# One fused compare-and-multiply on VectorE in the last attention batch, products on GpSimd elsewhere, and flags by maxima

## The chip, the cores and the metric

The kernel runs on one core of one Trainium2 chip. The metric is the device time in microseconds, the median of several executions. Engines are named as the profile does: PE is TensorE, DVE is VectorE, ACT is ScalarE, POOL is GpSimd, SP is the queue from which most transfers are issued.

## The reference

Four batches of eight heads, 576 positions and head size 64 go through attention that keeps the 32 largest scores of each row; its output (2304 rows of 512) goes through a mixture of eight experts, two for each row.

```python
scores = scale * np.matmul(q, k.transpose(0, 1, 3, 2))
kth = np.partition(scores, -32, axis=-1)[..., -32:-31]
scores = np.where(scores >= kth, scores, -1000000000.0)
attn = np.exp(scores - np.max(scores, axis=-1, keepdims=True))
attn = attn / (np.sum(attn, axis=-1, keepdims=True) + 1e-09)
x = np.matmul(attn, v)                                # then (2304, 512)
noisy = x @ w_gate + np.log1p(np.exp(x @ w_noise)) * noise
...                                                   # the two largest, softmaxed
out[mask] += top2_w[mask, k, None] * (np.maximum(x[mask] @ w1[e], 0.0) @ w2[e])
```

## The kernel before

**Attention.** A batch is 36 tiles of 128 query rows, 144 tiles in all (`attend`, `finish`, `gather`). For a tile, PE computes 576 scores in two halves (L577 for the first batch, L581 for the others), and ACT copies them to SBUF as `s` (L589). DVE folds the two halves into maxima and minima (L612) and finds the 32 largest in four rounds of eight (MAX8 at L616, with the found ones struck out at L621 between rounds). In some tiles (24 of 144, `DROPS`) ACT and POOL strike out the third eight; these leave one value each in `left` and `apart`. ACT takes the exponential of all scores, `es` (L644), which needs only the maximum; `es` has four buffers. The 32nd value decides which are kept: either DVE writes a mask `mk` of ones and zeros (`mask`, L648), or a threshold `under` (L678, on DVE or POOL) and a sign pass on ACT (L682) write it. `SIGNS` says how many tenths of the tiles of each batch take the second way: 10, 10, 6 and 4. Then `weigh` multiplies `es` by the mask (L693): on POOL, or on DVE where the planner finds that this is earlier by a margin (`WEIGHS`). POOL notes in `over` how the 32nd value stands to the rounds before (`note`, L696). PE transposes the product (L708, L712) and multiplies it with the values (L768, L770); ACT and DVE or POOL scale the rows by their sums (L789, L795, L803).

**Routing.** After each batch, `gate` computes the logits (L865, last part added by DVE at L881), and `route` computes gates, ranks and slots with small instructions on ACT, DVE and POOL; then ten indirect DMAs on POOL's queue scatter the rows into lists of each expert (L1044).

**Experts.** They run in three groups of rows: the first after batch 0, the second (256 rows of each expert) after batch 2, the third after batch 3. Each block of weights is loaded from HBM, rounded by ACT (`wh`, L1112), and the rest is taken by a subtraction on POOL or DVE (`wl`, L1116, 128x1024, two for each half-block). PE multiplies in three passes (L1200 to L1202 up, L1282 to L1284 down). Between the two, ACT writes the relu `hh` (L1206) and DVE the rest `hl` (L1210, a scalar_tensor_tensor with one operand in PSUM); for the inputs the same are L1170 and `xl` (L1173). An indirect DMA on POOL adds the result into the output (L1302). The experts of the second group are interleaved with the attention of the last batch.

**Order.** Each piece of work is a node with an engine, a duration, dependencies and a priority (low numbers first). `Plan.order` simulates the engines and lists the pieces in order of their planned start; each engine executes its own in that order. A node with `alt` may move to a second engine. Nodes with `lock=True` on DVE and POOL do not start in the plan while one of the other engine runs. Buffers are rings (`take`, `give`) that add dependencies.

**Flags.** Four reasons could make the fast path wrong; `bad` counts them, and at the end `bad` decides whether a general path runs instead. `flags(b)` (L1006 to L1020) counts them for one batch: for each of the three columns of `over`, for `under`, and for `left` and `apart` where the batch has any, a comparison into `fl` (L1018), a sum (L1019) and an addition to `bad` (L1020). That is 20 such groups. The four calls have the lowest priority of all and depend on every tile's note, so they come after the last tile.

Of the kernel before, what the change touches and what calls it, by code (L numbers as in the profile page):

```python
# [8 lines left out]
F32 = mybir.dt.float32  # L9
# [5 lines left out]
OP = mybir.AluOpType  # L15
# [16 lines left out]

SIGNS = (10, 10, 6, 4)


WEIGHS = (1500, 1600, 2300, 1900)
BIAS = (400, 300, 800, -1100)
BELOW = (1300, -2500, 2200, 2600)  # L40
LOWK = (2300, 400, 500, 1300)
# [17 lines left out]

TAKE = ((0, 208), (48, HS), (0, HS))  # L60
GLAG = 1

WHEN = (16, 15, -13, 0)

# [363 lines left out]
def sparse_attention_moe(ctx: ExitStack, tc: tile.TileContext, qk, v, wg, aux, noise, w1, w2, out):  # L428
# [62 lines left out]
    def qkv(n):  # L491
        b, h = divmod(n, H)

        def whole():
            hi[n] = P["hi"].tile([128, QW + KW], F32, name="hi", bufs=4)
            nc.sync.dma_start(hi[n][0:64], qk[b, h])
            vt[n] = P["v"].tile([128, 6, 65], F32, name="vt", bufs=NV)
            nc.sync.dma_start(vt[n], v[b, h])

        if b < NATIVE:  # L500
            a = add("SP", 1000, whole, move=1330, lat=700)
            QN[n] = (a, a, a, pl.take("hi", 4, a), None, pl.take("v", NV, a))
            return

        def load():
            raw[n] = P["raw"].tile([128, QW + KW], F32, name="raw", bufs=2)
            nc.sync.dma_start(raw[n][0:64], qk[b, h])
            nc.sync.dma_start(raw[n][64:128], qk[b, h])
            vt[n] = P["v"].tile([128, 6, 65], F32, name="vt", bufs=NV)
            nc.sync.dma_start(vt[n], v[b, h])  # L510

        def high():
            t = P["hi"].tile([128, QW + KW], F32, name="hi", bufs=4)
            hi[n] = t.bitcast(F32R)
            nc.scalar.activation(hi[n], raw[n], AF.Copy)

        def low_k(eng):
            kl[n] = P["kl"].tile([128, KW], F32R, name="kl", bufs=4)
            ENG[eng].tensor_tensor(kl[n], raw[n][:, QW:], hi[n][:, QW:].bitcast(F32), op=OP.subtract)

        def low_q(eng):
            ENG[eng].tensor_tensor(hi[n][64:128, :QW], raw[n][64:128, :QW], hi[n][64:128, :QW].bitcast(F32), op=OP.subtract)

        a = add("SP", 1500, load, move=2200, lat=2500)
        r, vv = pl.take("raw", 2, a), pl.take("v", NV, a)
        x = add("ACT", 1165, high, [a])
        hh = pl.take("hi", 4, x)
        y = add("POOL", 1545, low_k, [x], alt=("DVE", 736, LOWK[b]), lock=True)
        kk = pl.take("kl", 4, y)
        z = add("POOL", 1625, low_q, [x], alt=("DVE", 850, LOWK[b]), lock=True)  # L530
        pl.give(r, y, z)
        QN[n] = (a, y, z, hh, kk, vv)
# [18 lines left out]
    def attend(j):  # L551
# [129 lines left out]
            t["mk"] = W.tile([128, S], BF, name="mk", bufs=NMK)  # L681
            nc.scalar.activation(t["mk"], t["s"], AF.Sign, bias=under[:, j:j + 1])  # L682

        if sgn:
            k = add("DVE", 71, below, [d], alt=("POOL", 179, BELOW[b]))
            mk = add("ACT", 667, sign, [k])
        else:
            mk = add("DVE", 430, mask, [d], lock=True)
        bk = pl.take("mk", NMK, mk)
        pl.give(t["sbuf"], mk, x2)  # L690

        def weigh(eng):
            ENG[eng].tensor_tensor(t["e"], t["e"], t["mk"], op=OP.mult)  # L693

        def note():
            nc.gpsimd.tensor_tensor(over[:, j], t["t8"][:, 3, 7:8].to_broadcast([128, 3]), t["t8"][:, 0:3, 7], op=OP.subtract)  # L696

        w = add("POOL", 1240, weigh, [mk, x2], alt=("DVE", 669, WEIGHS[b]), lock=True)
        pl.give(bk, w)
        nt_ = add("POOL", 150, note, [mk])  # L700
        pl.give(b8, nt_, x1, k if sgn else mk, n2 or nt_)
        t["note"] = nt_

        def turn():
# [205 lines left out]
    def route(b):  # L910
# [92 lines left out]
                V.tensor_reduce(new("c0", [1])[:n], st["tm"][:n, 0, a:z, 8], axis=AX.X, op=OP.add)  # L1003
                V.tensor_tensor(bad[:n, 0:1], bad[:n, 0:1], st["c0"][:n], op=OP.add)

        def flags(b):  # L1006
            fl = R.tile([128, 36], F32, name="flg")
            fr = R.tile([128, 1], F32, name="fr")
            q = slice(b * 36, (b + 1) * 36)
            p = [sides.index(j) for j in range(b * 36, (b + 1) * 36) if j in sides]  # L1010
            p = slice(p[0], p[-1] + 1) if p else None
            for x, c, op in ((over[:, q, 0], 0.0, OP.is_gt), (over[:, q, 1], 0.0, OP.is_gt), (over[:, q, 2], 0.0, OP.is_gt),
                             (under[:, q], -2.0 ** -100, OP.is_gt), (left[:, p], HS - 15.0, OP.not_equal) if p else (None,) * 3,
                             (apart[:, p], 0.0, OP.is_le) if p else (None,) * 3):
                if x is None:
                    continue
                n = x.shape[1]
                nc.vector.tensor_scalar(fl[:, :n], x, c, None, op0=op)  # L1018
                nc.vector.tensor_reduce(fr, fl[:, :n], axis=AX.X, op=OP.add)  # L1019
                nc.vector.tensor_tensor(bad[:, 0:1], bad[:, 0:1], fr, op=OP.add)  # L1020

        x0 = add("ACT", 130, ex, [AVN["lgn", b]])
        pr = pl.take("route", 1, x0)
# [28 lines left out]

        for t in range(NT):
            for k in range(2):
                scat.append(add("POOL", 1280, scatter(t, k), [x, g, AVN["tok", b]] + [(s, True) for s in scat[-1:]] + FILLS, move=750, lat=700))
        y = add("DVE", 75, cnt, [x])
        ck = add("DVE", 1000, check, [x, od], prio=pl.prio + 150)
        if b == B - 1:
            for i in range(B):
                add("DVE", 2590, lambda i=i: flags(i), [T[j]["note"] for j in range(36 * B)], prio=10 ** 9)  # L1060
        pl.give(pr, x, y, ck, g)
        pl.give(AVN["xrp", b], scat[-1])
        pl.give(AVN["axp", b], x2, AVN["tok", b])
# [403 lines left out]
```

## Time and profile before

| what | us |
|---|---|
| median of 3 executions | 998.77 |
| lowest, highest | 997.01, 1000.16 |
| profiled execution, its own time | 1007.95 |
| its span, first to last instruction | 1006.2 |
| mean granted PE clock | 0.973 of full speed |

The profile is that of one execution, and the hardware profiler's times are of single instructions. The tiles of the last batch run from about 457 to 731 us of the span, its flags and routing after them up to about 773 us, and the rest is the end of the second and the third group of experts. The granted clock is a share of 2.4 GHz; about 0.5 is the lower level, 1.2 GHz.

### The profile page before, as it was taken

The numbers are of one execution on the slowest core, as the hardware profiler recorded it, in microseconds if no ns is written. First come the engines' busy times: TensorE is split into PE (matmuls) and PEld (weight loads), VectorE is DVE, ScalarE is ACT, GpSimd is POOL, SyncE is SP. The second block draws the span as 40 slices with busy tenths as digits, with TensorE's granted clock in tenths as the row PEclk, the third lists the DMA queues.
The fourth block names the chain that finished last, engine by engine and source line by source line (L and its number), as shares of the span: only waits on it lengthen the run. The fifth ranks groups of instructions, "written<-read, shape, count | busy, mean of one in ns | idle before, by whom it ended". The sixth has DMA issues, their size and how long they took to land.

```text
span 1006.2 us, 18439 instructions
## 1 busy us (share of the span) xinstructions
PE 940.1 (93%) x6160; PEld 788.6 (78%) x6176; DVE 695.3 (69%) x2190; ACT 680.0 (68%) x1533; POOL 742.4 (74%) x926
## 2 busy tenths in 40 slices
PE   9999998899999899999699999899978999999993
PEld 4777776787887677888489988799867888999892
DVE  6999998799999799999783578877784222222220
ACT  5888885688987478887476668577635555555550
POOL 4676677355657666677689889687858899999991
PEclk9999999799998999999999999999979999999997
DMA  9477222157366664566667677354556877776741
GB/s 281 162 259 258 49 70 93 28 155 214 125 175 175 234 172 113 154 188 149 217 231 220 168 199 191 96 159 137 137 158 206 245 215 232 233 226 211 230 126 25
DMA packets 109385, 173.92 MB, mean 173 GB/s; under 512 B 7648, under 2 KB 60896, under 8 KB 109280
## 3 DMA queue, kind: packets, MB, share of 16 engines
q1 hardware_dynamic: 100576, 152.42, 48.8%
q0 software_dynamic: 8704, 20.22, 9.7%
q8 instruction: 51, 0.84, 0.3%
q14 instruction: 54, 0.44, 0.1%
HBM read 136.34 MB, written 36.27 MB: 172 GB/s over the span
## 4 chain that ended last, share of the span: by engine, by line
PE 61%; DVE 11%; POOL 10%; ACT 7%; issue 5%; DMA 2%; another core or an unknown queue 1%; SPq 0%; POOLq 0%; DVEq 0%; ACTq 0%
PE bank L768 7%; PE hps L1200 4%; POOL wl L1116 4%; PE hps L1202 4%; PE hps L1201 4%; PE pp L708 4%; PE bk L577 4%; PE bk L581 4%; PE bk L1274 3%; PE bk L1284 3%; PE bk L1282 3%; DVE t L616 3%; PE bk L1283 3%; PE hps L1229 3%; PE hps L542 3%
## 5 line engine op out<-in xcount | busy, mean ns | idle before, releaser
L1116 POOL TENSOR_TENSOR wl<-wr,wh 128x1024 fp32r<-128x1024 f32 x118 | 292.6, 2717 | 26.6 <-ACT wh L1112 14.0
L616 DVE MAX8 t<-cat 128x8 f32<-128x288 f32 (+3 forms) x576 | 268.1, 490 | 9.4 <-POOL cat L630 6.7
L693 POOL TENSOR_TENSOR es<-es,mk 128x576 f32<-128x576 f32 x140 | 187.2, 1341 | 94.2 <-ACT mk L682 74.9
L1112 ACT ACTIVATE wh<-wr 128x1024 fp32r<-128x1024 f32 x128 | 133.7, 1056 | 51.1 <-PE bk L1284 25.4
L1210 DVE SCALAR_TENSOR_TENSOR hl<-hps,hh 128x256 fp32r<-128x256 f32 x128 | 53.8, 421 | 155.6 <-ACT hh L1206 152.8
L621 DVE MATCH_REPLACE8 cat<-t,cat 128x208 f32<-128x208 f32 (+2 forms) x408 | 159.9, 394 | 0.0
L1200 PE MATMUL hps<-xh,wh 128*128 128x256 f32 x512 | 149.9, 293 | 2.2 <-DVE hl L1210 2.2
L612 DVE TENSOR_TENSOR cat<-bk,s 128x288 f32<-128x288 f32 x288 | 125.5, 444 | 33.7 <-ACT s L589 33.5
L1202 PE MATMUL hps<-xh,wl 128*128 128x256 f32 x512 | 145.9, 285 | 0.5 <-POOL wl L1116 0.5
L1201 PE MATMUL hps<-xl,wh 128*128 128x256 f32 x512 | 145.8, 285 | 0.0
L768 PEld LDWEIGHTS bank<-vt,pt 128*128 128x128 f32 x1024 | 124.1, 196 | 15.1 <-ACT p L720 10.4
L768 PE MATMUL bank<-vt,pt 128*128 128x65 f32 x1024 | 126.3, 278 | 7.1 <-ACT p L720 7.0
L589 ACT ACTIVATE s<-bk 128x288 f32<-128x288 f32 x288 | 111.5, 416 | 31.8 <-PE bk L581 19.4
L644 ACT ACTIVATE es<-s,nb 128x576 f32<-128x576 f32 x144 | 111.7, 777 | 4.6 <-POOL nb L638 2.6
L716 ACT ACTIVATE pt<-pp 128x512 f32<-128x512 f32 x144 | 86.3, 599 | 33.8 <-PE pp L708 27.2
L1200 PEld LDWEIGHTS hps<-xh,wh 128*128 128x128 f32 x512 | 98.5, 192 | 4.6 <-DVE hl L1210 2.5
L1201 PEld LDWEIGHTS hps<-xl,wh 128*128 128x128 f32 x512 | 98.5, 192 | 2.0
L1202 PEld LDWEIGHTS hps<-xh,wl 128*128 128x128 f32 x512 | 98.3, 192 | 0.7 <-POOL wl L1116 0.7
L1206 ACT ACTIVATE hh<-hps 128x256 fp32r<-128x256 f32 x128 | 48.8, 381 | 70.6 <-PE hps L1202 66.2
L708 PE MATMUL pp<-ident,es 128*128 128x128 f32 x576 | 89.5, 278 | 7.1 <-POOL es L693 4.0
L682 ACT ACTIVATE mk<-s,under 128x576 bf16<-128x576 f32 x107 | 83.0, 780 | 16.4 <-POOL under L678 11.8
L581 PE MATMUL bk<-hi 128*128 128x288 f32 x240 | 90.0, 384 | 3.0 <-DVE cat L612 1.6
(155 smaller groups left out, 2048.0 us busy)
## 6 DMA issues: line engine op xcount, KB each, us to landing
wr<-in_w_dram SPq DMA_DIRECT2D x192, 512.0 KB, 4.7
raw<-in_qk_dram SPq DMA_DIRECT2D x48, 320.0 KB, 8.7
xg<-xs SPq DMA_DIRECT2D x16, 528.0 KB, 8.6
xs<-xg SPq DMA_DIRECT2D x16, 528.0 KB
vt<-in_v_dram SPq DMA_DIRECT2D x32, 195.0 KB, 6.3
out_dram<-xs SPq DMA_DIRECT2D x1, 5120.0 KB
hi<-in_qk_dram SPq DMA_DIRECT2D x8, 320.0 KB, 4.7
xg<-xs SPq DMA_DIRECT2D x8, 264.0 KB
```

The costliest lines, as they stand in the source:

```text
L581: nc.tensor.matmul(sp, lhs(n), rhs, start=(k == 0), stop=(k == 2 * len(heads) - 1))
L612: nc.vector.tensor_tensor(o, t["sp", 1], t["s"][:, :HS], op=op)
L616: return lambda: nc.vector.max(t["t8"][:, r], t["cat"] if r == 3 else t["cat"][:, slice(*TAKE[r])])
L621: nc.vector.match_replace(g, t["t8"][:, r], g, NEG)
L693: ENG[eng].tensor_tensor(t["e"], t["e"], t["mk"], op=OP.mult)
L708: nc.tensor.transpose(pp[:, c], t["e"][:, k0 + c * 128:k0 + (c + 1) * 128], ident)
L768: nc.tensor.matmul(accs[:, i + k], x["pt"][:, c], vt[n][:, c], start=(k + c == 0), stop=False, skip_group_check=True)
L1112: nc.scalar.activation(WS[n][0][:, i], W[n][:, i], AF.Copy)
L1116: return lambda eng: ENG[eng].tensor_tensor(WS[n][1][:, i], W[n][:, i], WS[n][0][:, i].bitcast(F32), op=OP.subtract)
L1200: nc.tensor.matmul(ps[:, :NN], ah, xh, start=(c == 0), stop=False)
L1201: nc.tensor.matmul(ps[:, :NN], ah, xl, start=False, stop=False)
L1202: nc.tensor.matmul(ps[:, :NN], al, xh, start=False, stop=(c == 3))
```

## The change

In batch 3 (`FUSED` has 10 tenths there and none elsewhere) one DVE instruction compares `s` with the 32nd value and multiplies by `es`, in place; no mask, no sign pass and no threshold are made there. In the other batches the product has POOL as its only engine. `flags` is called once: five reductions over all 144 tiles (the maximum of `over`, of `under` and of `left`, the minimum of `left` and of `apart`), then five one-element instructions that compare and add to `bad`. `SENDS` (all zeros) is added to the priority of the scatters.

```diff
+FUSED = (0, 0, 0, 10)
...
-WEIGHS = (1500, 1600, 2300, 1900)
...
+SENDS = (0, 0, 0, 0)
...
-        def low_k(eng):
+        def low_k(eng="POOL"):
...
-        if sgn:
-            k = add("DVE", 71, below, [d], alt=("POOL", 179, BELOW[b]))
-            mk = add("ACT", 667, sign, [k])
-        else:
-            mk = add("DVE", 430, mask, [d], lock=True)
-        bk = pl.take("mk", NMK, mk)
-        pl.give(t["sbuf"], mk, x2)
-
-        def weigh(eng):
-            ENG[eng].tensor_tensor(t["e"], t["e"], t["mk"], op=OP.mult)
+        def weigh():
+            nc.gpsimd.tensor_tensor(t["e"], t["e"], t["mk"], op=OP.mult)
+
+        def both():
+            nc.vector.scalar_tensor_tensor(t["e"], t["s"], t["t8"][:, 3, 7:8], t["e"], op0=OP.is_ge, op1=OP.mult)
+
+        if spread(j % 36, FUSED[b]):
+            k = w = mk = add("DVE", 690, both, [d, x2], lock=True)
+            pl.give(t["sbuf"], mk)
+        else:
+            if sgn:
+                k = add("DVE", 71, below, [d], alt=("POOL", 179, BELOW[b]))
+                mk = add("ACT", 667, sign, [k])
+            else:
+                k = mk = add("DVE", 430, mask, [d], lock=True)
+            bk = pl.take("mk", NMK, mk)
+            pl.give(t["sbuf"], mk, x2)
+            w = add("POOL", 1240, weigh, [mk, x2], lock=True)
+            pl.give(bk, w)
...
-        w = add("POOL", 1240, weigh, [mk, x2], alt=("DVE", 669, WEIGHS[b]), lock=True)
-        pl.give(bk, w)
         nt_ = add("POOL", 150, note, [mk])
-        pl.give(b8, nt_, x1, k if sgn else mk, n2 or nt_)
+        pl.give(b8, nt_, x1, k, n2 or nt_)
...
-        def flags(b):
...
+        def flags():
+
+            fr = R.tile([128, 5], F32, name="fr")
+            red = lambda k, x, op: lambda: V.tensor_reduce(fr[:, k:k + 1], x, axis=AX.XYZW if len(x.shape) > 2 else AX.X, op=op)
+
+            def sums():
+                for k, c, op in ((0, 0.0, OP.is_gt), (1, -2.0 ** -100, OP.is_gt), (2, HS - 15.0, OP.not_equal),
+                                 (3, HS - 15.0, OP.not_equal), (4, 0.0, OP.is_le)):
+                    V.scalar_tensor_tensor(bad[:, 0:1], fr[:, k:k + 1], c, bad[:, 0:1], op0=op, op1=OP.add)
+            notes = [T[j]["note"] for j in range(36 * B)]
+            fs = [add("DVE", 60 + n / .96, red(k, x, op), notes, prio=10 ** 9) for k, n, x, op in (
+                (0, 432, over.rearrange("p j k -> p (j k)"), OP.max), (1, 144, under, OP.max), (2, 40, left, OP.max),
+                (3, 40, left, OP.min), (4, 40, apart, OP.min))]
+            add("DVE", 600, sums, fs, prio=10 ** 9)
...
-                scat.append(add("POOL", 1280, scatter(t, k), [x, g, AVN["tok", b]] + [(s, True) for s in scat[-1:]] + FILLS, move=750, lat=700))
+                scat.append(add("POOL", 1280, scatter(t, k), [x, g, AVN["tok", b]] + [(s, True) for s in scat[-1:]] + FILLS,
+                                prio=pl.prio + SENDS[b], move=750, lat=700))
...
-            for i in range(B):
-                add("DVE", 2590, lambda i=i: flags(i), [T[j]["note"] for j in range(36 * B)], prio=10 ** 9)
+            flags()
```

## Rows read from the trace of the kernel before

**Rows 1.** The page, busy time of each engine

```profile
PE 940.1 (93%) x6160; PEld 788.6 (78%) x6176; DVE 695.3 (69%) x2190; ACT 680.0 (68%) x1533; POOL 742.4 (74%) x926
```

**Rows 2.** Windows: us, then busy PE, PEld, DVE, ACT, POOL; clock, DMA, GB/s

```profile
457.00:525.00 68.00, 59.22 (x373) 47.39 (x373) 55.78 (x184) 43.02 (x111) 48.93 (x74) 0.97 0.72 203
525.00:625.00 100.00, 98.00 (x705) 89.75 (x705) 61.19 (x176) 69.85 (x145) 89.62 (x75) 1.00 0.71 201
625.00:731.00 106.00, 100.46 (x719) 91.90 (x718) 85.81 (x219) 71.98 (x155) 85.87 (x81) 0.98 0.47 138
731.00:748.00 17.00, 11.26 (x71) 9.98 (x70) 15.56 (x58) 6.05 (x15) 9.58 (x8) 0.87 0.52 136
760.00:812.00 52.00, 47.84 (x305) 42.15 (x305) 14.05 (x28) 28.23 (x46) 46.74 (x42) 1.00 0.80 244
812.00:991.00 179.00, 177.11 (x1142) 159.44 (x1142) 37.55 (x89) 95.56 (x160) 164.98 (x102) 1.00 0.68 200
```

**Rows 3.** Chain of waits from 727 to 748 us, shares by line

```profile
by line: DVE bad L1020 49.0%; DVE fr L1019 18.7%; DVE flg L1018 15.2%; issue 6.6%; DVE hl L1210 5.2%; DVE xl L1173 3.1%; ACT hh L1206 1.9%; DVE lgs L881 1.1%; DVE rs L795 0.4%
```

**Rows 4.** Timeline of DVE and POOL during the flags: start, duration in us

```profile
727.74 0.75 DVE L1018 TENSOR_SCALAR flg<-over 128x36 f32<-128x36 f32 x1
...
729.78 2.18 DVE L1020 TENSOR_TENSOR bad<-bad,fr 128x1 f32<-128x1 f32 x1
...
732.31 1.96 DVE L1020 TENSOR_TENSOR bad<-bad,fr 128x1 f32<-128x1 f32 x1
...
741.31 3.56 DVE L1020 TENSOR_TENSOR bad<-bad,fr 128x1 f32<-128x1 f32 x1
...
747.22 0.16 DVE L1020 TENSOR_TENSOR bad<-bad,fr 128x1 f32<-128x1 f32 x1
...
729.55 4.71 POOL L1116 TENSOR_TENSOR wl<-wr,wh 128x1024 fp32r<-128x1024 f32 x2 [0.94 <-POOL over L696]
...
741.89 2.95 POOL L1116 TENSOR_TENSOR wl<-wr,wh 128x1024 fp32r<-128x1024 f32 x1
```

**Rows 5.** Timeline of PE during the flags: idle before, released by

```profile
735.65 0.44 PE L1166 MATMUL hps<-ident,xs 128*128 128x128 f32 x2 [1.73 <-DVE xl L1173]
...
748.28 0.80 PE L1284 MATMUL bk<-wh,hl 128*128 128x512 f32 x1 [4.29 <-DVE hl L1210]
```

**Rows 6.** Windows in which PE ran at the lower clock

```profile
736.50:740.20 3.70, 3.70 (x17) 3.37 (x16) 3.32 (x19) 2.33 (x4) 1.94 (x4) 0.54 0.80 264
748.30:754.00 5.70, 5.70 (x20) 5.08 (x21) 3.11 (x13) 0.70 (x3) 3.63 (x11) 0.52 0.44 157
```

**Rows 7.** Single lines: ns min/median/max, first and last start, forms

```profile
L1019 DVE TENSOR_REDUCE fr<-flg x20: 156/191/192, 728.5 to 747.0; 128x1 f32<-128x36 f32 x16, 128x1 f32<-128x21 f32 x2, 128x1 f32<-128x3 f32 x2
...
L693 DVE TENSOR_TENSOR es<-es,mk x4: 741/752/759, 164.2 to 338.4; 128x576 f32<-128x576 f32 x4
...
L1210 DVE SCALAR_TENSOR_TENSOR hl<-hps,hh x128: 400/425/427, 526.1 to 986.7; 128x256 fp32r<-128x256 f32 x128
...
L648 DVE TENSOR_SCALAR mk<-s,t x37: 490/510/2590, 302.3 to 724.0; 128x576 bf16<-128x576 f32 x37
```

**Rows 8.** Groups by line, 457 to 731 us: busy us, mean ns, idle before

```profile
L1116 POOL TENSOR_TENSOR wl<-wr,wh 128x1024 fp32r<-128x1024 f32 x44 | 110.3, 2573 | 20.9 <-ACT wh L1112 8.3 <-issue 8.1 <-POOL over L696 2.6
L693 POOL TENSOR_TENSOR es<-es,mk 128x576 f32<-128x576 f32 x38 | 53.4, 1407 | 14.8 <-DVE mk L648 7.3 <-ACT mk L682 6.3 <-PE bank L712 0.9
...
L648 DVE TENSOR_SCALAR mk<-s,t 128x576 bf16<-128x576 f32 x23 | 15.7, 686 | 0.2
```

**Rows 9.** Waits, 500 to 731 us: us in total, times, longest

```profile
PE pp L708 <- POOL es L693: 3.5, 4, 1.7
```

**Rows 10.** Timeline of POOL at the first scatter; window of L693 alone (DVE, POOL)

```profile
163.41 1.22 POOL L1044 DMA_INDIRECT xg<-xr,si  x1 [0.73 <-POOL spacer L1043]
...
175.17 0.91 POOL L1044 DMA_INDIRECT xg<-xr,si  x1 [0.25 <-issue]
...
160.00:200.00 40.00, 2.25 (x3) 3.85 (x3) 0.83 0.23 75
```

More of the change, by code (lines that the diff above doesn't have):

```diff
@@ L515, in high, with low_q @@
             nc.scalar.activation(hi[n], raw[n], AF.Copy)
-        def low_k(eng):
+        def low_k(eng="POOL"):
             kl[n] = P["kl"].tile([128, KW], F32R, name="kl", bufs=4)
             ENG[eng].tensor_tensor(kl[n], raw[n][:, QW:], hi[n][:, QW:].bitcast(F32), op=OP.subtract)
-        def low_q(eng):
+        def low_q(eng="POOL"):
             ENG[eng].tensor_tensor(hi[n][64:128, :QW], raw[n][64:128, :QW], hi[n][64:128, :QW].bitcast(F32), op=OP.subtract)
@@ L1004, in check @@
                 V.tensor_tensor(bad[:n, 0:1], bad[:n, 0:1], st["c0"][:n], op=OP.add)
-        def flags(b):
[L1007 to L1020, printed above, removed]
+        def flags():
[10 more added lines that the diff above has]
+            add("DVE", 600, sums, fs, prio=10 ** 9)
         x0 = add("ACT", 130, ex, [AVN["lgn", b]])
```

## The prediction

> **What bounds the kernel now.** I read the busy line of the page first, then a table by stage, then the chain of waits where TensorE stands, and last the single instructions. TensorE is busy 940.1 of 1006.2 us [rows 1]: over the whole span it is the bound, and a change pays by the TensorE idle time and half-clock time that it takes away. The table by stage [rows 2] says where these are: of the last batch of attention (457 to 731 us) TensorE is idle 8.8 us in the first stretch, 2.0 in the second and 5.5 in the third; in 731 to 748 it is idle 5.7 of 17 us; then 4.2 us from 760 to 812, and 1.9 of the next 179. VectorE, which the change loads, is busy 202.8 of the 274 us of the last batch, so it has 71 us to spare; GpSimd is busy 224.4 there.
>
> Between 727 and 748 us the chain of waits is VectorE's, and 82.9% of it are the three lines of the flag counts [rows 3]: 17.4 of 21 us. The instructions run from 727.74 to 747.38 without a gap, and three of them last 2.18, 1.96 and 3.56 us where most last 0.16; the last two end, to 0.03 us, where GpSimd's subtractions (L1116) end, at 734.26 and 744.84, and the first near the middle of the pair of them that began at 729.55 [rows 4]. Behind them on VectorE's queue stand the low parts that TensorE needs: it waits 1.73 us for xl and 4.29 us for hl [rows 5]. After each wait TensorE runs at its lower level, 1.2 GHz: granted 0.54 over 3.70 us and 0.52 over 5.70 us [rows 6], which costs 3.70 x 0.46 + 5.70 x 0.48 = 4.4 us.
>
> **The flags.** Removed: 20 groups of three instructions. Added: five reductions and five one-element updates of `bad`. A reduction took 156 ns at 3 elements and 191 at 36 [rows 7], about 1.06 ns an element, so 432 elements take 0.61 us, 144 take 0.31 and three of 24 (the width of `left` and `apart`) 0.18 each: 1.5 us. The updates depend on each other; at 0.2 us from one to the next they add 1.0. The stretch shrinks from 17.4 to 2.5 us if no update meets GpSimd, and to 2.5 + 7.2 = 9.7 if three still do, as now (the excess of the three over 0.16 us). I take one meeting, 2 us, so 4.5, since five updates offer fewer chances than twenty. On TensorE the stretch is worth at most 1.73 + 4.29 + 4.4 = 10.4 us; with what one meeting leaves I take **8 us**. The end of the route (gates, ranks, scatters) moves up by about as much, because the last logits also queue behind the flags; so the last experts' weights, which GpSimd prepares after the scatters, move with it and do not become the next wait at once.
>
> **The last batch.** Removed: 22 masks on VectorE, 14 sign passes on ScalarE with their 14 thresholds, 36 products on GpSimd. In the table of lines the masks are 15.7 us (23 of them in this window) and the products 53.4 us at 1407 ns [rows 8]. Added: 36 instructions of 128x576 with two operands in SBUF. No row has that form. The bounds: the same product on VectorE took 752 ns, and the same operation over 256 elements took 425 [rows 7]; adding 320 elements at 1.06 ns to the latter gives 0.76. So 36 x 0.76 = 27.4 us in, 15.7 out: VectorE gains 11.7 us of its 71 idle. GpSimd loses 36 x 1.4 = 50 us. What TensorE can surely get of that is what its matmuls waited for the product: 3.5 us [rows 9]. Against it stands one new wait: the fused instruction needs the exponential as well as the thresholds, and on VectorE's queue it holds up hl and xl behind it, which TensorE waits for; before, only GpSimd's queue held it. From zero (covered by the idle 71 us) to what the first rival prices. I take 0.5 us for this, and 3.5 for the gain: **3 us**, of 7.5 idle in 525 to 731.
>
> The transposes follow the fused instruction directly, so the last tile's product no longer stands behind two subtractions on GpSimd; TensorE has expert work meanwhile, so this alone is worth nothing to it. The scores, loads and expert instructions are the same in number. `SENDS` is all zeros and moves no scatter; the default of `eng` in low_k and low_q is overridden by the planner. A plan made anew can still shift orders everywhere: zero in the sum, up to 3 us either way in the range.
>
> **The four products that leave VectorE.** Three of the four fall into 160 to 200 us, the first scatter [rows 10]. The scatters hold GpSimd from 163.41 to 176.08, and their planner value goes before that of the next tiles' products. The first of them, which began at 164.2 on VectorE [rows 7], now waits until about 176.1: 11.9 us for that tile, less for the others. It saves VectorE 4 x 0.75 = 3 us. Between a gain of 3 and a loss of 11.9 I take a loss of **1 us**: four buffers of `es` let the next tiles go on meanwhile.
>
> **The sum.** 8 + 3 - 1 = 10 us. The profiled execution took 1007.95 us with a span of 1006.2, and would take 998. It is 9.2 us above the median of the runs, 998.77, which by the same difference becomes 988.8: **989 us**.
>
> **Rivals.** First, **VectorE stands at the shared port**, and the kernel is slower. The row for it: two-operand updates with both inputs in SBUF waited for L1116 to end [rows 4]; the instruction with one input in PSUM never exceeded 427 ns in 128 runs [rows 7]. The fused instruction has both in SBUF. L1116 holds 110.3 of 274 us on GpSimd [rows 8]: 40%. A fused instruction that falls in at random waits 0.4 x 2.573/2 = 0.51 us, so 36 of them 18.5 us. Against: the plan keeps the two apart, and the masks, which show blocking too (686 ns in the mean [rows 8] against a median of 510, the longest 2590 [rows 7]), lost only about 4 us in 23. If 18.5 us reach TensorE, the kernel takes 989 + 18.5, about 1007. It decides from (8 + 3 - 1)/36 = 0.28 us for each fused instruction that TensorE has to wait. The Trainium skill, in "SBUF — State Buffer", section "Who interferes with whom", states this lock: a VectorE instruction with two SBUF inputs contends with a GpSimd instruction that reads SBUF, and the later one is blocked until the other has ended. The trace agrees: the three long updates end with L1116 [rows 4]. By that rule alone, without the plan's order, the sum would be a loss of 8 us.
>
> Second, **the scatters take it back**: the whole 11.9 us at 164 us reach the end, against 11 of gain: about 1000, no change. For it: no expert work exists yet there with which TensorE could fill the wait. Against: the four buffers, and the 3 us that VectorE saves.
>
> Third, **the flags are hidden anyway**: TensorE finishes the second group's experts sooner and then waits for the third group's weights, since GpSimd is busy 46.7 of 52 us from 760 to 812 [rows 2]. Then the 8 us reappear as idle time at about 800, and the change is worth 2: 997. Against: the route moves up with the flags.
>
> **Chances.** The forecast, 0.73; the port, 0.14; scatters or hidden flags, 0.13 together. A measurement tells 0.3% (3 us) from no change: faster 0.73, same 0.13, slower 0.14. Low end: all idle and half clock from 525 to 748 goes, 7.5 + 10.4, and the plan gives 2 more: 979. High end: the scatter rival with 2 us of a shifted plan, 1002; the port's worst case lies outside.
>
> **What would show it.** Right: ten flag instructions in under 6 us instead of 60 in 19; TensorE idle in the 17 us after the last tile under 2 us, and no half clock there; the last L616 followed by an instruction of about 0.76 us; GpSimd's busy time some 40 us lower; from 812 to the end the same duration. Wrong: fused instructions with a mean over 1.05 us that end with L1116, and more waits of L1284 for hl; TensorE idle over 12 us between 160 and 200; a new gap before the first expert of the last group.

## The result: 1.3% slower, and the profile after

The changed kernel takes 1009.65 us (median of 7 runs, 1003.75 to 1015.81), the kernel before 997.80 in the same session (7 runs, 995.02 to 1000.16). The ratio is 1.0129 with an interval of 1.0092 to 1.0165: some 13 us slower, where 989 us was forecast. Its profiled execution took 1014.31 us with a span of 1012.0; before, 1007.95 and 1006.2. The two profiles differ by only 5.8 us because the profiled execution of before lay 10 us above its median.

The busy line of the page, after:

```profile
PE 945.0 (93%) x6167; PEld 793.6 (78%) x6183; DVE 702.4 (69%) x2148; ACT 673.3 (67%) x1520; POOL 703.7 (70%) x881
```

GpSimd lost the forecast 40 us (742.4 in [rows 1]). TensorE has as many instructions to run as before but is busy 4.9 us longer: that is time at the lower clock (granted 0.967 over the span, 0.973 before). Windows of the kernel after, columns as in [rows 2]:

```profile
160.00:200.00 40.00, 36.88 (x229) 27.32 (x231) 34.99 (x126) 24.03 (x61) 27.79 (x51) 0.96 0.24 82
...
457.00:525.00 68.00, 58.12 (x345) 47.69 (x344) 57.63 (x172) 40.17 (x101) 35.22 (x57) 0.88 0.59 182
525.00:625.00 100.00, 96.23 (x659) 87.84 (x658) 67.70 (x177) 62.42 (x131) 70.52 (x58) 0.95 0.66 191
625.00:737.00 112.00, 102.44 (x728) 93.39 (x727) 94.83 (x230) 72.07 (x158) 79.78 (x66) 0.98 0.47 139
737.00:766.00 29.00, 27.73 (x207) 25.16 (x206) 14.69 (x39) 14.41 (x28) 20.09 (x26) 1.00 0.42 123
766.00:819.00 53.00, 49.11 (x297) 43.94 (x296) 15.79 (x32) 26.96 (x45) 42.73 (x42) 0.94 0.77 244
```

For each stretch I add TensorE's idle time and what the clock kept back (length times one minus the granted clock, taken before it is rounded to the two digits of the rows), in both traces, with the stretches of the kernel after set 6 us later from 731 on:

| stretch | lost before, us | lost after, us | difference |
|---|---|---|---|
| 0 to 160 | 3.4 | 3.3 | -0.1 |
| 160 to 200, first scatter | 12.6 | 4.8 | -7.7 |
| 200 to 457 | 17.6 | 20.1 | +2.5 |
| last batch, from 457 to 731 (737) | 19.7 | 38.6 | **+18.8** |
| the 29 us after the last tile | 12.0 | 1.3 | **-10.7** |
| from there to the end | 27.9 | 32.1 | +4.2 |

The differences add up to 7.0 us, the spans differ by 5.8. So the flags gave what was forecast in their own stretch, and the last batch lost what the first rival named. Groups by line of the kernel after, 457 to 737 us, the fused instruction (L690) and GpSimd's weight subtraction (L1124, before L1116):

```profile
L1124 POOL TENSOR_TENSOR wl<-wr,wh 128x1024 fp32r<-128x1024 f32 x47 | 116.9, 2544 | 39.1 <-ACT wh L1120 36.8 <-issue 2.2
...
L690 DVE SCALAR_TENSOR_TENSOR es<-s,t,es 128x576 f32<-128x576 f32 x36 | 46.6, 1303 | 0.2
```

The median of the fused instruction is 0.81 us, its mean 1.303: 36 x (1.303 - 0.80) = 18.1 us of standing still, in eleven instructions. What TensorE waited for in that stretch (total, times, longest):

```profile
PE pp L717 <- DVE es L690: 10.7, 4, 4.4
PE hps L1208 <- DVE hl L1218: 6.1, 4, 3.0
```

The transposes (L717) waited 3.5 us for the product [rows 9]; now they wait three times as long for what replaced it. The longest case, in the timelines of VectorE, GpSimd and TensorE:

```profile
673.37 5.80 DVE L690 SCALAR_TENSOR_TENSOR es<-s,t,es 128x576 f32<-128x576 f32 x1
...
673.37 2.73 POOL L1124 TENSOR_TENSOR wl<-wr,wh 128x1024 fp32r<-128x1024 f32 x1
675.72 0.53 POOL L707 TENSOR_TENSOR over<-t 128x3 f32<-128x3 f32 x1
675.87 2.67 POOL L1124 TENSOR_TENSOR wl<-wr,wh 128x1024 fp32r<-128x1024 f32 x1
...
679.31 1.09 PE L717 MATMUL pp<-ident,es 128*128 128x128 f32 x4 [4.44 <-DVE es L690]
```

Two subtractions that stand one behind the other end at 678.54; 0.63 us later, four fifths of an undisturbed length, the fused instruction is done. It did not get in between the two. The transposes after it took 1.09 us for the 0.60 of an undisturbed group: the lower clock.

The flags in VectorE's timeline:

```profile
736.00 0.59 DVE L1018 TENSOR_REDUCE fr<-over 128x1 f32<-128x432 f32 x1
736.50 0.29 DVE L1018 TENSOR_REDUCE fr<-under 128x1 f32<-128x144 f32 x1
...
736.97 0.93 DVE L1023 SCALAR_TENSOR_TENSOR bad<-fr,bad 128x1 f32<-128x1 f32 x5
```

Ten instructions in 1.9 us take the place of 60 in 19.6 [rows 4]; no update met GpSimd.

### The profile page after: what moved, and what is told of

The parts are those of the page before. It is cut to its first block, busy times and chain, and to the rows that moved or that the text cites. A ratio compares the mean times of both kernels' runs of the same rounds, so it can differ in the third digit from the quotient of the medians.

```text
span 1012.0 us, 18339 instructions
## 1 busy us (share of the span) xinstructions
PE 945.0 (93%) x6167; PEld 793.6 (78%) x6183; DVE 702.4 (69%) x2148; ACT 673.3 (67%) x1520; POOL 703.7 (70%) x881
## 4 chain that ended last, share of the span: by engine, by line
PE 62%; DVE 16%; POOL 7%; ACT 6%; issue 4%; DMA 2%; another core or an unknown queue 2%; SPq 0%; POOLq 0%; DVEq 0%; ACTq 0%
PE bank L777 7%; PE hps L1208 5%; PE hps L1210 5%; DVE t L618 5%; PE hps L1209 5%; PE pp L717 4%; PE bk L579 4%; PE bk L583 3%; DVE cat L623 3%; PE bk L1290 3%; PE bk L1282 3%; PE bk L1291 3%; PE bk L1292 3%; POOL wl L1124 3%; PE hps L1237 3%
## 5 line engine op out<-in xcount | busy, mean ns | idle before, releaser
L1124 POOL TENSOR_TENSOR wl<-wr,wh 128x1024 fp32r<-128x1024 f32 x121 | 298.8, 2700 | 52.1 <-ACT wh L1120 49.8
L687 POOL TENSOR_TENSOR es<-es,mk 128x576 f32<-128x576 f32 x108 | 142.9, 1328 | 68.8 <-ACT mk L684 58.8
L1218 DVE SCALAR_TENSOR_TENSOR hl<-hps,hh 128x256 fp32r<-128x256 f32 x128 | 53.9, 421 | 150.7 <-ACT hh L1214 144.6
L777 PEld LDWEIGHTS bank<-vt,pt 128*128 128x128 f32 x1024 | 125.0, 196 | 18.6 <-ACT p L729 10.7
L717 PE MATMUL pp<-ident,es 128*128 128x128 f32 x576 | 90.1, 280 | 12.7 <-DVE es L690 10.7
L717 PEld LDWEIGHTS pp<-ident,es 128*128 128x128 f32 x576 | 69.0, 144 | 32.8 <-issue 17.4
```

Of the source, the lines that this page charges most:

```text
L687: nc.gpsimd.tensor_tensor(t["e"], t["e"], t["mk"], op=OP.mult)
L717: nc.tensor.transpose(pp[:, c], t["e"][:, k0 + c * 128:k0 + (c + 1) * 128], ident)
L777: nc.tensor.matmul(accs[:, i + k], x["pt"][:, c], vt[n][:, c], start=(k + c == 0), stop=False, skip_group_check=True)
L1124: return lambda eng: ENG[eng].tensor_tensor(WS[n][1][:, i], W[n][:, i], WS[n][0][:, i].bitcast(F32), op=OP.subtract)
```

## Experiments

Every ratio is to the kernel before, run between on the same chip; the runs were spread over four chips.

### Is it the port?

**One input from SBUF.** In the changed kernel:

```diff
-  nc.vector.scalar_tensor_tensor(t["e"], t["s"], t["t8"][:, 3, 7:8], t["e"], op0=OP.is_ge, op1=OP.mult)
+  nc.vector.match_replace(t["e"], t["t8"][:, 3], t["e"], NEG)
```

> The changed kernel, in which the fused instruction is replaced by a match-replace over es alone (576 elements, one operand in SBUF, nothing found to replace), at the same place of the plan, so that the attention of the last batch keeps all 576 weights. Every engine's order stays the same. Port theory: the instruction lasts about 0.8 us each time, the 18 us by which the 36 fused ones exceed 0.8 us are gone, and the time falls from 1010 to 992 to 998 us. Rival (a longer VectorE queue and a worse plan, whatever the operands): the time stays within 3 us of 1010.

Measured: 0.9885 (0.9827 to 0.9942), 24 us below the changed kernel. Its group on VectorE, 457 to 737 us, the window, and the same wait of TensorE:

```profile
L690 DVE MATCH_REPLACE8 es<-t,es 128x576 f32<-128x576 f32 x36 | 26.6, 742 | 0.0
...
457.00:737.00 280.00, 266.74 (x1863) 239.80 (x1861) 208.84 (x634) 184.42 (x410) 185.77 (x189) 0.98 0.60 174
```

```profile
PE pp L717 <- DVE es L690: 2.6, 2, 1.6
```

No excess is left, and the wait is down from 10.7 to 2.6 us. In this trace TensorE loses 20.1 us in the last batch (counted as in the table of the result), where the changed kernel lost 38.6 and the kernel before 19.7. GpSimd did exactly the same work at the same places of its queue. The exchange also changes the operation; but the same operation with its first operand in PSUM (`hl`, L1218) never exceeded 0.427 us in its 128 runs in the changed kernel. So what the fused instruction loses, it loses through its second operand in SBUF.

**GpSimd's pieces halved.** In the changed kernel, between the first and the last fused instruction:

```diff
-                return lambda eng: ENG[eng].tensor_tensor(WS[n][1][:, i], W[n][:, i], WS[n][0][:, i].bitcast(F32), op=OP.subtract)
+                def fn(eng):
+                    for q in (slice(0, 512), slice(512, 1024)) if pl.halves else (slice(0, 1024),):
+                        ENG[eng].tensor_tensor(WS[n][1][:, i, q], W[n][:, i, q], WS[n][0][:, i, q].bitcast(F32), op=OP.subtract)
...
```

> Edit: the changed kernel with its plan as it is, but between the first and the last fused instruction each subtraction of weights (128x1024) is issued as two of 128x512. Theory A: a fused instruction waits for the rest of the one GpSimd instruction that runs, and takes the port at its end: half the length, half the excess, so 18.1 us over 0.80 each falls to 8 to 10 us, the longest fused instruction from 5.80 to under 2.5 us, and the time by 6 to 10 us, ratio 1.003 to 1.007. Theory B: GpSimd keeps the port through instructions that stand ready one behind the other (the 5.80 us one stood through two): the excess stays 15 to 20 us, the longest over 4 us, the ratio 1.010 to 1.017. If the waits were not the port's but VectorE's own, the excess would stay too, but without the ends of the fused instructions falling on ends of L1124.

Measured: 1.0187 (1.0131 to 1.0243). The fused instruction as a single line (ns min/median/max), and the longest case in VectorE's, GpSimd's and TensorE's timelines:

```profile
L690 DVE SCALAR_TENSOR_TENSOR es<-s,t,es x36: 796/810/7540, 461.6 to 731.5; 128x576 f32<-128x576 f32 x36
```

```profile
598.78 7.54 DVE L690 SCALAR_TENSOR_TENSOR es<-s,t,es 128x576 f32<-128x576 f32 x1
...
600.09 3.04 POOL L1126 TENSOR_TENSOR wl<-wr,wh 128x512 fp32r<-128x512 f32 x2
602.52 0.75 POOL L707 TENSOR_TENSOR over<-t 128x3 f32<-128x3 f32 x1
602.68 3.02 POOL L1126 TENSOR_TENSOR wl<-wr,wh 128x512 fp32r<-128x512 f32 x2
...
606.38 1.12 PE L717 MATMUL pp<-ident,es 128*128 128x128 f32 x4 [6.09 <-DVE es L690]
```

The numbers are theory B's, with the ratio just above its range: the mean is 1.33 us, as large as with whole pieces, and one fused instruction stood 7.54 us, from 598.8, through a whole row of half pieces. But B's reason holds only in part, for a boundary between two ready GpSimd instructions does let VectorE in at times. In the changed kernel, GpSimd and VectorE, each instruction by itself:

```profile
707.80 2.40 POOL L1124 TENSOR_TENSOR wl<-wr,wh 128x1024 fp32r<-128x1024 f32 x1 [2.13 <-ACT wh L1120]
...
709.58 1.24 DVE L690 SCALAR_TENSOR_TENSOR es<-s,t,es 128x576 f32<-128x576 f32 x1
...
710.16 2.92 POOL L1124 TENSOR_TENSOR wl<-wr,wh 128x1024 fp32r<-128x1024 f32 x1
```

The fused instruction waited for the first subtraction and ended 0.62 us after it; the second lasted 2.92 us where 2.40 is the median. In four traces (the changed kernel, this one, and below the alternative kept and the old order) fused instructions stood waiting at 26 boundaries of two subtractions and were let in at 10 of them. At 13 of the 16 others the profile has the second subtraction start more than 0.2 us before the first has ended, and at none of the 10. Why it starts so early there is not shown. [rows 4] had such a case already: the update of 2.18 us ended in the middle of a pair of subtractions. Halving also made the work longer: GpSimd was busy 125.0 us with the 94 halves, against 116.9 with 47 whole pieces.

**The alternative kept, and GpSimd held back.** The changed kernel with the products of the first three batches free to go to VectorE as before; then the same with a real dependency, so that GpSimd's next long instruction waits for the fused one:

```diff
+WEIGHS = (1500, 1600, 2300, 1900)
...
-            w = add("POOL", 1240, weigh, [mk, x2], lock=True)
+            w = add("POOL", 1240, weigh, [mk, x2], alt=("DVE", 669, WEIGHS[b]), lock=True)
...
+            r = x.fn()
+            if x.fn.__name__ == "both":
+                fused = r
+            elif fused is not None and x.eng == "POOL" and x.lock:
+                after(tc, r, fused)
+                fused = None
```

> The changed kernel with the second engine for the product given back in batches 0 to 2 (WEIGHS as before): so the new flags and the fused instruction, without the moved products. If the three parts add: the flags' -11, the fused instruction's +12, so 0.998 to 1.004 of before. If the moved products did not cost by themselves (another plan by chance): 1.01 or more. The fused instruction still shows its wait for GpSimd, a mean of about 1.3 us.

> The kernel of e5 with the plan's order between the two engines made real: after each fused instruction, the next GpSimd piece that the plan locks waits for it to be done. Port theory: GpSimd has idle time there, so the fused instruction's mean falls from 1.3 towards 0.9 us and the time to between 0.975 and 0.99 of before. Rival: GpSimd then hands its wait on to the low parts of the weights, and TensorE waits for these: no faster than e5.

Measured: 1.0062 (1.0019 to 1.0106) and 1.0006 (0.9966 to 1.0045). The fused instruction, 457 to 737 us, first without and then with the dependency:

```profile
L691 DVE SCALAR_TENSOR_TENSOR es<-s,t,es x36: 786/807/9476, 457.8 to 728.5; 128x576 f32<-128x576 f32 x36
```

```profile
L691 DVE SCALAR_TENSOR_TENSOR es<-s,t,es x35: 786/809/2937, 457.1 to 713.3; 128x576 f32<-128x576 f32 x35
```

The first ratio lies between its two expectations and decides for neither. One fused instruction stood 9.48 us. Held back, GpSimd can make it wait only for the piece that already runs: the longest is 2.94 us, and the excess over 0.80 falls from 16.3 to 7.5 us. The time falls by 0.6%, which the two intervals hardly tell from none, and ends level with the kernel before, not 1 to 2.5% below it as the port theory expected here.

### What are the flags worth?

**The new flags alone**, in the kernel before: the hunks of `flags`, `sums` and the call from the diff, no other. Run twice.

> The kernel before with the new flags alone. If the flags bounded the stretch behind the last tile, as forecast: 988 to 992 us, with the scatters of the last batch about 7 us earlier. Rival (something else in that stretch ends as late, so the flags are hidden): 995 to 999.

> The run with the new flags alone once more, beside the two others: it should repeat 0.984 to 0.994 if the worth of the flags under the old plan is no chance of one chip or hour; over 0.996 would say that the spread between runs is as large as what is told here.

Measured: 0.9888 (0.9836 to 0.9941), and 0.9945 (0.9906 to 0.9985) the second time, a hair beyond what it was to repeat: 5 to 11 us gained.

**The old flags in the changed kernel**: those hunks undone.

> The changed kernel with the old flags. If the new flags are worth 8 us there: 1016 to 1020. If they are hidden behind another wait in the changed kernel: 1007 to 1013.

Measured: 1.0117 (1.0078 to 1.0157) against 1.0129: no gain to be told. Yet in the traces the gain is there. From the start of the tiles' last MAX8 to the end of the span it is 285.9 us with the old flags and 279.8 with the new, 6.1 less (in the kernel before 284.5, with the new flags alone 277.3: 7.2 less). Up to the last tile TensorE has the same order in both programs, and the fused instructions wait alike (TensorE waits 10.7 us in four times for them in each trace), but the one with the new flags came to that point 7.1 us later: between 484 and 530 us TensorE lost 18.0 us in it and 9.7 in the other, and 6.8 of the difference is clock. That scatter is as large as the effect.

**The old flags under another order**: the kernel before with a product planned 1250 instead of 1240 ns long.

> Edit: the kernel before with its old flags; the planned length of a product 1250 instead of 1240 ns. With the new flags this plan gave 0.9988. If the new flags are worth their 8 to 11 us in any plan, this one gives 1.007 to 1.011. If their worth hangs on what the plan puts behind the last tile (in the changed kernel they were worth nothing), 0.998 to 1.003.

Measured: 1.0105 (1.0059 to 1.0151). With the new flags the same order gave 0.9988 (next section): 12 us.

### What does an order made anew cost?

**Not fused**: the changed kernel with `FUSED = (0, 0, 0, 0)`. **Products moved** in one batch: the kernel before with the new flags and `alt=None` where `b == 1`. **Another plan**, with nothing moved: the same with 1250 for the planned length. **A third plan**: with 1230.

> The changed kernel with FUSED all zeros: masks as before in the last batch, all products on GpSimd, new flags. Port theory: the fused instruction carries the whole loss, so the time is that of the flags alone within 3 us. Rival (the products moved to GpSimd at the first scatters carry it): 1003 or more, with TensorE idle over 12 us between 160 and 200 us.

> The kernel of e2 (new flags alone) with the three products of batch 1 that the plan gave to VectorE on GpSimd. If the products cost at their place or through the plan that follows from them: 8 to 12 us over e2, 0.997 to 1.001 of before. If they cost nothing and something else in e3 does: within 3 us of e2, 0.986 to 0.992.

> The kernel of e2 with the planned length of the product at 1250 in place of 1240 ns: not one instruction more or less, or on another engine's account by intent, but a plan made anew, with about half as many lines in another place as e7 has. If a plan's luck is worth about 1%: 5 us or more from e2 either way. If not: within 3 us of e2, and then the products' place counts.

> Edit: the kernel before with the new flags; the planned length of a product 1230 instead of 1240 ns, nothing else: the planner makes another order from the same work (the order of the matrix multiplications differs more from the first than that of the run with 1250). If plans differ by about 1% from one to another, this one falls anywhere from 0.985 to 1.005. If the first plan is a picked one and others cost some 10 us, 0.997 to 1.005. If 1250 was the odd one, 0.986 to 0.992, as with the new flags alone.

Measured: 1.0005 (0.9967 to 1.0044), 0.9994 (0.9962 to 1.0026), 0.9988 (0.9950 to 1.0025) and 1.0137 (1.0085 to 1.0189), all with the new flags, which in the first order give 0.9888 and 0.9945. Ten nanoseconds in one planned length are worth 0.4 to 2.5%. So the 5 to 12 us by which the first two lie above the flags alone say nothing about where the products run: the third pays as much without moving one.

### The fused instruction in the old order

The new flags in the kernel before, its plan untouched; in the last batch the mask's place issues the fused instruction, and products and masks are left out. Then the same with the instruction of one input, and with GpSimd held back as above:

```diff
+        def both():
+            t["two"] = t.get("two", 0) + 1
+            if b == 3 and t["two"] == 2:
+                nc.vector.scalar_tensor_tensor(t["e"], t["s"], t["t8"][:, 3, 7:8], t["e"], op0=OP.is_ge, op1=OP.mult)
```

> Edit: the kernel before with the new flags, its plan untouched, so that every engine keeps the order of the run with the new flags alone; only in the last batch the mask's place issues the fused instruction (or the exponential's, where that comes later), and the products of GpSimd and the masks of ScalarE are left out. So the fused instruction comes in without a plan made anew and without moved products. Port theory: the fused instructions wait for L1116 as in the changed kernel, 12 to 20 us over 0.80 us each, against some 4 to 8 us of waits for products and masks that go; with the flags' -11 us the ratio to the kernel before is 0.993 to 1.004, and the fused group's mean lies over 1.1 us. If all of the changed kernel's loss is the fused instruction and none of it the new plan, 1.010 or more. If the loss was the new plan's alone, the fused instruction helps or does nothing here: 0.985 to 0.989, mean 0.80 to 0.9 us.

> Edit: as the run with the fused instruction in the old order (0.9979), but the fused instruction is a MATCH_REPLACE8 of the exponentials that reads one operand from SBUF beside its 8 values; every engine's order is that run's. The last batch then keeps all 576 weights. If what the fused instruction costs there (0.9888 to 0.9979) is the wait for GpSimd's port less a relief by the products and masks that go (about 11 us, from the two runs under the new plan with and without it), the ratio is 0.973 to 0.983, below the flags alone. If the relief belongs to the new plan and not to the fused instruction, 0.986 to 0.992. If the instruction's loss in this order were not the port, 0.995 to 1.001.

> Edit: as the run with the fused instruction in the old order, and GpSimd's next long instruction after each fused one (by the program's order) waits for it. Output is the reference's. Port theory: only a GpSimd instruction that already runs can hold the fused one up; under the other plan that took the excess from 16.3 to 7.6 us and 0.6% of the time, so here 0.988 to 0.994, with a longest fused instruction under 3.5 us. If GpSimd's time is what bounds the batch, the added waits cost it: over 1.000. This is the candidate that would beat the flags alone if it comes to under 0.985.

Measured: 0.9979 (0.9939 to 1.0019), 0.9813 (0.9764 to 0.9861), 0.9859 (0.9803 to 0.9914). The first one's fused instruction by line, 457 to 729 us, TensorE's largest wait there, and its longest case in VectorE's and TensorE's timelines:

```profile
L650 DVE SCALAR_TENSOR_TENSOR es<-s,t,es 128x576 f32<-128x576 f32 x34 | 46.1, 1364 | 1.1 <-ACT es L644 1.0
```

```profile
PE bk L1298 <- DVE hl L1224: 5.7, 4, 4.2
```

```profile
653.15 5.79 DVE L650 SCALAR_TENSOR_TENSOR es<-s,t,es 128x576 f32<-128x576 f32 x1
658.86 0.41 DVE L1224 SCALAR_TENSOR_TENSOR hl<-hps,hh 128x256 fp32r<-128x256 f32 x1
...
659.33 0.78 PE L1298 MATMUL bk<-wh,hl 128*128 128x512 f32 x1 [4.21 <-DVE hl L1224]
```

The fused instructions stand as long as in the changed kernel, 34 x (1.364 - 0.80) = 19.2 us, and no transposes wait for one. The stall reaches TensorE through hl, which stands behind it on VectorE's queue. From one input to two it costs 0.9979 - 0.9813, 16.6 us, in this order; in the new one 1.0129 - 0.9885, 24.4. Each of the two is good to some 6 or 7 us. What masks and products cost before, and the fused instruction saves, is 0.9813 against 0.9888 or 0.9945, 7 to 13 us. With GpSimd held back the kernel leaves nothing out and is 1.4% faster than before: the best of the orders tried, though its interval overlaps that of the flags alone. In its trace the longest fused instruction lasts 3.35 us and the excess is 12.7 us.

### ScalarE's stalls

The traces differ in one more row. ScalarE's timeline, the kernel before and then the kernel after, only the instructions that stood still for something that no engine of this core does:

```profile
177.93 0.60 ACT L716 ACTIVATE pt<-pp 128x512 f32<-128x512 f32 x1 [5.88 <-remote]
...
492.23 0.39 ACT L1233 ACTIVATE hl<-hps 128x256 f32<-128x256 f32 x1 [4.41 <-remote]
```

```profile
178.37 0.71 ACT L591 ACTIVATE s<-bk 128x288 f32<-128x288 f32 x2 [6.63 <-remote]
...
499.08 0.38 ACT L1241 ACTIVATE hl<-hps 128x256 f32<-128x256 f32 x1 [3.97 <-remote]
```

They add up to 17.3 us before and 17.6 after, but to 3.8 in the run with the fused instruction in the old order. Nearly all lie in the scatters, and at the same counts of ScalarE's instructions whatever instruction that is. But the place does not make the stall by itself. With GpSimd held back ScalarE has the same instructions in the same order as in that run, and after its 355th, with the first scatter under way in both, it stood 5.71 us; in that run 1.54 (the first line below). The run with one input in the old order has no such stall there either.

```profile
171.76 0.60 ACT L730 ACTIVATE pt<-pp 128x512 f32<-128x512 f32 x1 [1.54 <-issue]
...
177.83 0.60 ACT L730 ACTIVATE pt<-pp 128x512 f32<-128x512 f32 x1 [5.71 <-remote]
```

To move the places, 48 instructions were put ahead of it, in the kernel before and in the changed one:

```diff
+    few = cp.tile([1, 1], BF, name="few")
+    for _ in range(48):
+        nc.scalar.activation(few, C["dummy"][:1], AF.Copy)
```

> Edit: the kernel before with 48 one-element activations ahead of ScalarE's work, nothing else; they go by while ScalarE has little to do, in the first 15 us. In the kernel before ScalarE stands still four times, 17.3 us in all, for something that no engine of this core does (5.88 us before 177.93, 3.74 before 337.34, 4.41 before 492.23, 3.26 before 499.47), each time inside the scatters. In the traces of 16 kernels the first such stall comes at ScalarE's instruction 355 or 348 and nowhere else, whatever that instruction is, the next ones near 665 and 962: a place in its stream of code. Theory C, code that comes late while the scatters load the DMA engines: 48 instructions move the places some 24 us forward, out of the scatters; the waits fall from 17 to under 5 us and the time by 6 to 15 us, ratio 0.985 to 0.994. Theory S, ScalarE waits for something of the scatters themselves: the stalls stay at 172 to 178 us, now at instruction 403, ratio 0.997 to 1.005. If one place is only swapped for another, 0.995 to 1.003 with stalls elsewhere.

> Edit: the changed kernel with the same 48 one-element activations. Its stalls of this kind are 17.6 us; in the run with the fused instruction in the old order they were 3.8 us, and that run was 15 us faster. Theory C: what was put down to the new plan is mostly these stalls, so the ratio to the kernel before falls from 1.0129 to 0.998 to 1.006, with the excess of the fused instructions still 16 to 20 us. If the new plan itself costs the 15 us (transposes planned closer behind the fused instruction), it stays at 1.009 to 1.016.

Measured: 1.0081 (1.0042 to 1.0121) and 1.0122 (1.0087 to 1.0157). Neither trace has a stall of this kind any more. The first stretches of the kernel before with the 48:

```profile
0.00:20.00 20.00, 16.80 (x43) 6.73 (x44) 9.85 (x41) 16.02 (x64) 6.35 (x25) 0.83 0.95 275
160.00:200.00 40.00, 38.66 (x267) 28.74 (x269) 38.64 (x139) 29.58 (x73) 27.41 (x56) 1.00 0.24 81
```

In 160 to 200 us TensorE lost 1.3 us, not 12.6. But the 48 were not free: they took 9.7 us in the first 20, and the first scatter began 12.0 us later (175.4 against 163.4; 4.0 in the changed kernel). So the stalls went when their places moved, as theory C has it, but its forecast of the time failed twice. What the stalls cost stays open: the changed kernel did not come down against the kernel before, yet with the 48 in both it is only 0.4% slower (1.0122 against 1.0081), and no run tells how much of that is the price of the 48. Nor does the trace show late code. The page of the kernel before has two queues of instructions, and none of their 105 packets starts within one of its four stalls:

```profile
q8 instruction: 51, 0.84, 0.3%
q14 instruction: 54, 0.44, 0.1%
```

## Why the prediction was wrong

**The flags (8 us): right.** The ten instructions took less than the 4.5 us allowed for them, and 10.7 of the 12.0 us that TensorE lost in that stretch are gone, its clock full. After 766 us it lost 4.2 us more than before, which may be part of what the third rival said; at the end they are worth 5 to 12 us in three comparisons, and nothing that could be told in the changed kernel.

**The last batch (3 us): this step failed**, at "I take 0.5 us for this". The new wait was put between zero and the first rival's price and taken near zero, because 71 idle us of VectorE would cover it and "the plan keeps the two apart". Neither held. The stalls met instructions that TensorE was waiting for, whatever VectorE idled at other times. And the plan keeps the two engines apart only in its own planned times, in which the fused instruction has 690 ns: nothing in the program makes one wait for the other. The rows at hand spoke for the rival: three flag updates out of twenty had waited until a GpSimd subtraction ended [rows 4], and the nearest form in operands was that one, not the mask with its one wide input, on which the counterargument rested. The rival's price, 18.5 us, met the excess of 18.1: 11 of the 36 waited, 1.6 us in the mean, where it had 40% and 1.29, and only one of them longer than one piece. That the batch's +18.8 us is the same number is in part luck: 6.9 of it is idle time of TensorE and 11.9 its clock, and not every stall reached TensorE. In time the second operand cost 24.4 us in this order and 16.6 in the old one. The rule of the Trainium skill that the prediction quoted ("SBUF — State Buffer", section "Who interferes with whom") stood on the right side, and the run with one input shows its condition, the second input from SBUF, in this kernel.

**The relief (3.5 us): too small.** Taking masks and products away is worth 7 to 13 us in the old order; between two new orders, with them and without, it was 12 (1.0005 and 0.9885), which an order alone can be worth. Only the waits that the trace put down to the product were counted; that the rest lies in VectorE's and ScalarE's own queues is argued, not shown.

**Four products (-1 us): cannot be told.** The second rival's loss did not show: TensorE lost 7.7 us less in 160 to 200 us and 2.5 more in the next 257, so 24.9 us in both against 30.2 before. But the two traces of the flags alone, in which VectorE still has these products, lost 26.3 and 24.8 there.

**"A plan made anew": zero, up to 3 us either way: this failed too.** The same work in other orders differed by up to 2.5%. In the sum of the measured ratios the fused instruction and the flags come to 0.9979 in the old order, so 15 us of the changed kernel's loss belong to its order, each ratio good to some 4 to 6 us. These 15 split into 8 because the same port stalls cost more in it (24.4 against 16.6) and 7 without any port (0.9885 against 0.9813); neither part alone is clear of noise, with intervals of 9 and 8 us either way. For the 8 the rows have a reason: in the new order the transposes wait for the fused instruction itself, 10.7 us, and in the old one not at all. That they stand too close behind it because the plan expects 690 ns is argued, not tried. For the 7 no cause was found; ScalarE's stalls are not excluded.

## What to carry to other kernels

Before a VectorE instruction gets a second operand in SBUF, count how long GpSimd is busy beside it: the price here was half of one GpSimd instruction's length times GpSimd's share, for each instruction, and it came in few, long stalls (11 of 36) that also held up what stood behind. When an edit makes a planner lay out everything anew, measure a second order of unchanged work first: here it moved the time more than the edit did. Test the parts of such a change in the old order, one by one.

## What the runs showed of the hardware that was not expected

- A VectorE instruction that waits for the port can stand through several GpSimd instructions that are ready one behind the other: 5.80 us through two, 9.48 through a running subtraction and three more, 7.54 through half pieces. At 10 of 26 boundaries it was let in between two, and at none of the 13 where the profile has the second start more than 0.2 us before the first has ended. Half pieces did not lower the waits here; a dependency that holds GpSimd back did (longest 2.94 us, and 3.35 in the old order).
- ScalarE stood still up to 7.29 us at fixed places of its instruction stream (355, about 665, about 962) in most traces in which these fell into a scatter, and nowhere once they were moved. That its code comes late then is one reading; no row shows the code arriving. The Trainium skill, in "Runtime: NRT & Kernel Launch", section "Instruction fetch mechanics", says that an engine streams its code in blocks through a DMA queue and that this is mostly hidden; no run here shows that it was not hidden.
- Two programs with one order on TensorE up to the last tile (the changed kernel with the new flags and with the old) differed by 7.1 us there in their profiles, mostly through the clock: after the same wait of 3.11 us for a fused instruction it cost one 3.4 us and the other nothing.
